# A fused retention and expert kernel: first values by a second queue, the first expert's start moved into the last tiles, rank tables moved later

## The chip, the cores and the metric

One core of one Trainium2 chip. Its engines are named as the profile names them: PE is TensorE (matrix products), PEld its weight loads, DVE is VectorE, ACT is ScalarE, POOL is GpSimd, and SP issues most DMAs. The metric is the device time of one execution in microseconds (us).

## The reference

```python
# attention: 8 batches x 8 heads x 576 positions x 64
scores = (1/sqrt(64)) * q @ k^T
ret    = (scores * gamma[h] ** (i - j) where i >= j, else 0) @ v
x      = ret as [4608 tokens, 512]
# experts: 4 groups of 4, one of 16 for each token
g_idx  = argmax(x @ w_group);          g_w = its softmax weight
e_idx  = argmax(x @ w_expert[g_idx]);  e_w = its softmax weight
out[token] = g_w * e_w * (relu(x[token] @ w1[g, e]) @ w2[g, e])   # 512 -> 1024 -> 512
```

All in float32. Each token goes to exactly one of the 16 experts.

## The kernel before, in words

The work has two phases. In the first, 36 tiles of 128 tokens (`NT`) pass through the attention. For a tile t, `loads` brings `a` (q and k, transposed) and `b` (k and v), 512 KB each, six tiles ahead; `scale` multiplies the values by the decay on ACT (`vs`); `scores` makes `pss`, which DVE masks into `sT`; `av` makes `px` from `sT` and `vs`; `state` adds to the running state `pst`, copied to `st` by ACT; `inter` adds the state's share to `px`; `turned` scales it on DVE into `xT`, the tokens in transposed form. Tiles are routed in groups of three (`RG`): `logits` (`plt`), `gate_pe` (transposed logits, `pl`), `choose` (a chain of small DVE operations from `lg` to `ob`, the chosen expert as a one-hot row), `places_pe` and `places` (the row in the expert's list, `sl`), `weigh` (the gate weight, `wt`). `xnat` then transposes a tile back (`pxt`), scales it (`xt`) and scatters its rows to the expert's list `xs` in DRAM, by an indirect DMA of POOL.

In the second phase the experts follow one another, in order of their token counts. Pass p has eight steps f: `layer1` makes a 128-wide piece `ph` of the hidden layer, ACT makes `hh` of it, and `layer2` of the step before adds to the outputs `py`. Weights come in four pieces for each expert (`load_piece`, two DMAs `r` of 512 KB). They and the tokens are split into a high and a low part (`wh` on ACT, `wl` on DVE) for three products; the first six steps of pass 0 use whole float32 weights instead (`whole`). `xload` reads an expert's tokens from `xs` (`xb`, four DMAs and the ids) and must wait until all scatters so far have landed, that of `xpad` (rows of zeros behind the list) too. `xturn` transposes them on DVE (`xTf`), `xsplit` splits them (`xTh`, `xTl`). The outputs are transposed on DVE (`yturn`) and scattered by POOL (`ystore`, `finish`).

The first expert is chosen before all tiles are counted: `PICK` is tile 26, and with r = t - 26 the loop calls `pick(0)` at r = 5, `taken` and `xload(0)` at r = 6 and the weights' pieces at r = 6 to 9. Its first 256 tokens (`EARLY`) are pass 0; the rest of its tokens are a last pass 16. The remaining routing of the last tiles is mixed into pass 0, and `rank_experts` ranks all experts by count in three parts, taken one at a time by `next(ranks, None)`.

The order of the work on every engine is the order in which the code calls it: `Ordered` pins each instruction behind the one before on its engine. What is written in another order runs in another order. Only the reads of a register (`expert_of`) aren't pinned. Every recorded operation has the line of that helper, L117, so the rows are read by the names of tiles.

```python
        Ordered.on = True
        act.dma_start(cf[:, 0:KC_UP], c_f[:, 0:KC_UP])
        act.activation(warm, warm, AF.Exp)
```

Of the kernel before, what the change touches and what calls it, by code (L numbers as in the profile page):

```python
# [15 lines left out]
P = 128  # L16
# [50 lines left out]
def moe_retention(ctx, tc, qk, kv, wgt, w1, w2, c_f, out):  # L67
# [262 lines left out]
    def xnat(t):  # L330
        xnat_pe(t)
        xnat_out(t)
        xnat_store(t)

    def xnat_pe(t):

        T = tiles[t]
        T["pxt"] = ps_tr.tile([P, NKC, P], F32, name=f"pxt_{t}", tag="tr")
        for i in range(NKC):
            pe.transpose(T["pxt"][:, i, :], T["xT"][:, i, :], ident)  # L340
# [181 lines left out]

    obs = []
# [3 lines left out]
    with ExitStack() as ac:  # L527
# [7 lines left out]
        def loads(t, nms):  # L535
# [52 lines left out]
        for t in range(LOADS - 1):  # L588
# [137 lines left out]
        for t in range(NT + 1):  # L726
# [22 lines left out]
            if t:  # L749
                inter(t - 1)  # L750
                turned(t - 1)
# [6 lines left out]
            if now and 6 <= t:  # L758
# [9 lines left out]
            u = t - 6  # L768
# [3 lines left out]
            for u in range(max(u + 1, 0), t - 5):  # L772
# [74 lines left out]

    def layer1(p, f):
        i = p * NPIECE + f // 2
        C = CS[p]  # L850
        if (p, f) == (0, 0):
            ph = ps_st.tile([P, CMAX], F32, name=f"ph_{p}_{f}", tag="tr")
        elif p == 0:
            ph = psy.tile([P, CMAX], F32, name=f"ph_{p}_{f}", tag=f"py{f % 2}")
        else:
            pool_ = (ps_sm, ps_tr, ps_sm, ps_st)[f % 4]
            ph = pool_.tile([P, CMAX], F32, name=f"ph_{p}_{f}", tag="sm" if f % 2 == 0 else "tr")
        cs = slice((f % 2) * P, (f % 2) * P + P)
        hh = mp.tile([P, CMAX], F32R, name=f"hh_{p}_{f}", tag="hh", bufs=4)
        if whole(p, f):  # L860
            for kc in range(NKC):
                pe.matmul(
                    ph[:, :C], raws[i][0][:, kc, cs], xTf[p][:, kc, :C], start=kc == 0, stop=kc == NKC - 1
                )
            act.activation(hh[:, :C].bitcast(F32), ph[:, :C], AF.Relu)
            hts[p, f] = (hh.bitcast(F32), None)
            return
        wh, wl = wsp[i, 0]
        xh, xl = xTs[p]
        n = 0  # L870
        for kc in range(NKC):
            for a, b in ((wh, xh), (wh, xl), (wl, xh)):
                pe.matmul(
                    ph[:, :C], a[:, kc, cs], b[:, kc, :C], start=n == 0, stop=n == 3 * NKC - 1
                )
                n += 1
        C32 = 32 * nblocks(p)
        if f == 0 and C32 > C and not natural(p):

            dve.memset(hh[:, C:C32].bitcast(F32), 0.0)  # L880
        hl = mp.tile([P, CMAX], F32R, name=f"hl_{p}_{f}", tag="hl", bufs=4)
        act.activation(hh[:, :C], ph[:, :C], AF.Relu)
        dve.scalar_tensor_tensor(
            hl[:, :C], ph[:, :C], 0.0, hh[:, :C].bitcast(F32), ALU.max, ALU.subtract
        )
        hts[p, f] = (hh, hl)
# [98 lines left out]
    for p in range(E):  # L985
        for f in range(NFC):
# [5 lines left out]
            for i in new:  # L992
                if i not in raws and (i >= len(pieces) or pieces[i][0] in ereg):
                    load_piece(i)
            layer1(p, f)
            if (p, f) == (0, 0):
# [370 lines left out]
```

## Time and profile before

| | |
|---|---|
| three runs | 609.99 us median, 607.59 to 610.55 |
| the profiled execution | 606.85 us |
| its span, first to last instruction | 605.1 us |
| PE busy | 584.0 us, 97% of the span |
| DVE, ACT, POOL busy | 430.2, 325.2, 263.3 us |
| mean DMA rate | 237 GB/s |

A share of the span is an average over stages with different limits. Here PE is nearly always busy; where it is not, the wait has to be looked up at its place. Stretches of the timeline are given in us from the start of the span: the tiles take the first 150 us, pass 0 lasts until about 182, the last pass begins at about 584.

### The profile page before, as it was taken

Reading aid. Unit: us, or ns where it says so; the run is one execution under the profiler, and the core shown is the slowest. Engines: PE = TensorE matmul, PEld = TensorE weight load, DVE = VectorE, ACT = ScalarE, POOL = GpSimd, SP = SyncE. Lnnn points to the kernel's source line nnn. Section 1 sums busy time; section 2 is a strip of 40 time slices with the busy share of each in tenths; the row PEclk is TensorE's granted clock in tenths of the full one; section 3 lists DMA queues with packets and bytes.
Section 4 is the critical chain, followed back from the end, with each engine's and each line's share of the span. In section 5 each row is a group of like instructions: output and inputs, shape, how many; then the busy total and the mean of one; then the engine's idle time right before and its main releaser. Section 6 shows DMA issues by size and latency. Waiting matters only on the chain.

```text
span 605.1 us, 16614 instructions
## 1 busy us (share of the span) xinstructions
PE 584.0 (97%) x6191; PEld 549.7 (91%) x6191; DVE 430.2 (71%) x977; ACT 325.2 (54%) x849; POOL 263.3 (44%) x392
## 2 busy tenths in 40 slices
PE   7889999998999999999999999999999999999995
PEld 7778788777668999999999999999999999999994
DVE  3777677677477666997757675867768677686773
ACT  4677877865346434445435454544545455455553
POOL 0022322333313037494645537373563734636554
PEclk8999999999999999999999999999999999999999
DMA  8999999956983942819465563838467394674921
GB/s 332 416 384 341 344 344 337 353 183 194 381 261 97 349 199 77 298 40 340 111 265 146 230 235 145 284 115 311 130 245 249 123 334 118 259 240 153 369 93 35
DMA packets 62546, 143.11 MB, mean 237 GB/s; under 512 B 9313, under 2 KB 30185, under 8 KB 62464
## 3 DMA queue, kind: packets, MB, share of 16 engines
q1 hardware_dynamic: 53072, 121.59, 57.1%
q0 software_dynamic: 9248, 20.35, 9.4%
q8 instruction: 49, 0.80, 0.5%
q14 instruction: 33, 0.27, 0.1%
q10 hardware_dynamic: 144, 0.10, 0.1%
HBM read 121.67 MB, written 24.88 MB: 242 GB/s over the span
## 4 chain that ended last, share of the span: by engine, by line
PE 87%; DMA 5%; DVE 2%; issue 2%; POOL 1%; ACT 1%; SPq 0%; POOLq 0%; ACTq 0%; DVEq 0%
PE py L117 34%; PE ph L117 34%; PE px L117 7%; PE pss L117 4%; PE pxt L117 3%; PE pst L117 2%; DMA b<-in_kv 2%; PE plt L117 2%; POOL out L117 1%; DMA r<-in_w 1%; DMA xb<-xs 1%; DMA a<-in_qk 1%; PE pl L117 1%; DMA xs<-xt,sl 1%; PE phn L117 0%
## 5 line engine op out<-in xcount | busy, mean ns | idle before, releaser
L117 POOL DMA_INDIRECT out<-y,ii x152 | 167.2, 1100 | 51.0 <-issue 33.8
L117 DVE TENSOR_TENSOR wl<-r,wh 128x512 fp32r<-128x512 f32 x260 | 167.8, 687 | 8.3 <-ACT wh L117 4.5
L117 ACT ACTIVATE hh<-ph 128x356 fp32r<-128x356 f32 (+16 forms) x128 | 53.8, 420 | 212.6 <-PE ph L117 143.1
L117 PE MATMUL ph<-xTh_m,wh 128*128 128x356 f32 (+15 forms) x488 | 147.5, 302 | 0.8 <-ACT xTh_m L117 0.8
L117 ACT CAST wh<-r 128x512 fp32r<-128x512 f32 x260 | 146.9, 617 | 0.0
L117 PE MATMUL ph<-xTl_m,wh 128*128 128x356 f32 (+15 forms) x488 | 146.7, 301 | 0.1
L117 PE MATMUL ph<-xTh_m,wl 128*128 128x356 f32 (+15 forms) x488 | 146.6, 300 | 0.0
L117 PE MATMUL py<-hh,wh 128*128 128x288 f32 (+17 forms) x480 | 145.1, 302 | 0.0
L117 PE MATMUL py<-hl,wh 128*128 128x356 f32 (+14 forms) x480 | 144.7, 301 | 0.0
L117 PE MATMUL py<-hh,wl 128*128 128x356 f32 (+14 forms) x480 | 144.6, 301 | 0.0
L117 DVE SCALAR_TENSOR_TENSOR hl<-ph,hh 128x356 fp32r<-128x356 f32 (+15 forms) x122 | 56.7, 465 | 103.0 <-ACT hh L117 69.9
L117 POOL COPY pace<-hh 1x1 f32<-1x1 f32 x140 | 34.6, 247 | 140.4 <-ACT hh L117 138.4
L117 PEld LDWEIGHTS ph<-xTh_m,wh 128*128 128x128 f32 x488 | 92.0, 189 | 1.7 <-ACT xTh_m L117 1.2
L117 PEld LDWEIGHTS ph<-xTl_m,wh 128*128 128x128 f32 x488 | 92.0, 189 | 0.9 <-DVE xTl_m L117 0.4
L117 PEld LDWEIGHTS ph<-xTh_m,wl 128*128 128x128 f32 x488 | 92.2, 189 | 0.0
L117 PEld LDWEIGHTS py<-hh,wh 128*128 128x128 f32 x480 | 90.5, 189 | 0.2
L117 PEld LDWEIGHTS py<-hl,wh 128*128 128x128 f32 x480 | 90.4, 188 | 0.2 <-DVE hl L117 0.2
L117 PEld LDWEIGHTS py<-hh,wl 128*128 128x128 f32 x480 | 90.5, 189 | 0.0
L117 POOL DMA_INDIRECT xs<-xt,sl x36 | 35.9, 998 | 119.5 <-DVE ob L117 47.1
L117 ACT ACTIVATE vs<-b,cf 128x64 f32<-128x64 f32 x288 | 72.4, 335 | 7.9 <-DMA b<-in_kv 7.9
L117 DVE TENSOR_TENSOR sT<-pss,masks 128x512 f32<-128x512 f32 x72 | 46.0, 681 | 15.9 <-PE pss L117 10.7
L117 PE MATMUL px<-sT,vs 128*64 128x128 f32 x576 | 40.1, 280 | 2.2 <-DVE xT L117 1.7
(167 smaller groups left out, 615.8 us busy)
## 6 DMA issues: line engine op xcount, KB each, us to landing
r<-in_w SPq DMA_DIRECT2D x138, 512.0 KB
a<-in_qk SPq DMA_DIRECT2D x35, 512.0 KB
b<-in_kv SPq DMA_DIRECT2D x35, 512.0 KB
xb<-xs SPq DMA_DIRECT2D x24, 148.5 KB
xb<-xs SPq DMA_DIRECT2D x20, 165.0 KB
out<-y,ii POOLq DMA_INDIRECT x152
xb<-xs SPq DMA_DIRECT2D x12, 181.5 KB
xb<-xs SPq DMA_DIRECT2D x4, 198.0 KB
```

The costliest lines, as they stand in the source:

```text
L117: i_ = f(*a, **k)
```

## The change

It moves work; no product is added or removed.

- Start: the first tile's values (`b` of tile 0, two DMAs) are issued by ACT instead of SP, the second half first. The factors `gqs` go behind tile 1's loads, the gate's weights `wgp` and the second part of the constants `cf` behind tile 3's.
- Choice of the first expert: tile 26's `xnat` moves to r = 5, ahead of `pick(0)`'s product, into another PSUM pool. Weight pieces are loaded at r = 5 to 8, the first ahead of the tokens' read; the tokens are transposed at r = 8.
- First product: `layer1(0, 0)` moves into the loop, between tile 34's `inter` and `turned`. Its `hh` lies in a weight buffer. `layer1` itself moves up in the file.
- Pass 0: the routing of the last tiles is distributed otherwise over its steps; `layer2(0, 5)` goes ahead of `layer1(0, 6)`; the padding for the second expert is scattered before the last two tiles.
- Second and third part of the ranking move to the steps (1, 0) and (1, 1), and with them `ids(1)`, `xpad(2)` and `xload(2)`.
- End: one more split of the last pass's weights is called ahead of the last full pass's `layer2`.

```diff
+    def xnat_pe(t, pool_=None):
+        T["pxt"] = (pool_ or ps_tr).tile(
+            [P, NKC, P], F32, name=f"pxt_{t}", tag="sm" if pool_ else "tr"
+        )
...
+        if (p, f) == (0, 0):
+            hh = wp.tile([P, NKC, EARLY], F32, name="hh_0_0", tag="wl0", bufs=3)[:, 0]
...
                     for i in range(2):
-                        sp.dma_start(T[nm][:, i], src[nm][t, :, i])
+                        if nm == "a":
+                            sp.dma_start(T[nm][:, i], src[nm][t, :, i])
+                        else:
+                            act.dma_start(T[nm][:, 1 - i], src[nm][t, :, 1 - i])
...
-            if t == 0:
+            if t == 1:
                 sp.dma_start(gqs[0], c_f[:, KC_GQ:KC_ALL].rearrange("p (x j) -> p x j", x=4))
-            if t == 1:
+            if t == 3:
                 sp.dma_start(wgp, wgt.rearrange("p (c e) -> p c e", c=NKC))
                 sp.dma_start(cf[:, KC_UP:KC], c_f[:, KC_UP:KC])
...
                 inter(t - 1)
+                if r == 9:
+                    layer1(0, 0)
                 turned(t - 1)
...
-            if now and 6 <= t:
+            if now and 6 <= t and r != 6:
                 xnat_pe(t - 6)
                 xnat_out(t - 6)
...
+            if r == 5:
+                xnat_pe(PICK, ps_sm)
+                xnat_out(PICK)
             if now and last_of_group(t - 4):
                 places_pe(t - 4)
...
-            if r in (6, 7, 8, 9):
+            if r in (5, 6, 7, 8):
                 if r == 6:
                     xload(0)
-                load_piece(r - 6)
-            if r == 9:
+                load_piece(r - 5)
+            if r == 8:
                 xturn(0, 0, 2)
                 xturn(0, 1, 2)
...
+            ahead = (p, f) == (0, WHOLE)
+            if ahead:
+                layer2(*prev)
             layer1(p, f)
-            if (p, f) == (0, 0):
+            if (p, f) == (0, 1):
                 places_pe(NT - 4)
                 places(NT - 4)
                 logits(NT - 1)
                 xnat(NT - 6)
-                xnat(NT - 5)
-                gate_pe(NT - 1)
                 pick(1)
-            if (p, f) == (0, 1):
                 expert_of(1)
-                choose(NT - 1)
+            if (p, f) == (0, 2):
                 xnat(NT - 4)
-            if (p, f) == (0, 2):
                 places_pe(NT - 1)
                 places(NT - 1)
                 weigh(NT - 1)
-                xnat(NT - 3)
             if (p, f) == (0, 3):
-                xnat(NT - 1)
+                xnat(NT - 2)
+                count_experts()
+                xnat(NT - 1, ps_sm)
                 xload(1)
...
+            if (p, f) == (0, 1):
+                gate_pe(NT - 1)
+                choose(NT - 1)
+                xnat(NT - 5)
             if (p, f) == (0, 2):
+                xnat(NT - 3)
                 tiles_counted()
-                xnat(NT - 2)
-                count_experts()
-            if (p, f) in ((0, 4), (0, 5)):
+            if (p, f) in ((0, 4), (1, 0), (1, 1)):
                 next(ranks, None)
...
+            if (p, f) == (1, 1):
+                ids(1)
...
+            if (p, f) == (1, 2):
+                xpad(2)
+            if (p, f) == (1, 3):
+                xload(2)
...
         if pc == 0:
 
+            split(2 * E * NPIECE + 3)
             layer2(*prev)
...
-            split(2 * (E * NPIECE + pc) + 3 + k)
+            split(2 * (E * NPIECE + pc) + 4 + k)
```

On SP, at the start of the program, the first loads stand in this order; a and b are a tile's two loads (a_134 and b_136 of before are a_133 and b_135 now, tile 1), gq, wgp and cf the constants.

```order
-L117 DMA b_130<-in_kv 128x512 x2
+L117 DMA a_133<-in_qk 128x1024
+L117 DMA b_135<-in_kv 128x1024
 L117 DMA gq_113<-c_f 128x512
-L117 DMA a_134<-in_qk 128x1024
-L117 DMA b_136<-in_kv 128x1024
+L117 DMA a_138<-in_qk 128x1024
+L117 DMA b_140<-in_kv 128x1024
+L117 DMA a_142<-in_qk 128x1024
+L117 DMA b_144<-in_kv 128x1024
 L117 DMA wgp<-in_wgt 128x128
 L117 DMA cf<-c_f 128x517
```

Tile 0's b is gone from SP, gq stands behind tile 1, and wgp and cf stand behind tiles 2 and 3.

On PE, from tile 34's first product on, before:

```order
L117 MATMUL px_3089<-sT_2979,vs_2917 64x128 x8
L117 MATMUL px_3089<-a_2456,st_2943 64x128 x8
L117 MATMUL pxt_3107<-cf,xT_2494 128x128 x4
L117 MATMUL pl_3114<-cf,lt_3075 128x128 x3
L117 MATMUL px_3145<-sT_3060,vs_3006 64x128 x8
L117 MATMUL px_3145<-a_2537,st_2652 64x64 x8
L117 MATMUL px_3145<-a_2537,st_3032 64x64 x8
L117 MATMUL ph_0_3193<-xTf_3128,r_0_0_2899 128x256 x4
```

and now:

```order
L117 MATMUL px_3098<-sT_2983,vs_2921 64x128 x8
L117 MATMUL px_3098<-a_2456,st_2947 64x128 x8
L117 MATMUL ph_0_3115<-xTf_3095,r_0_0_2824 128x256 x4
L117 MATMUL pxt_3123<-cf,xT_2494 128x128 x4
L117 MATMUL pl_3130<-cf,lt_3079 128x128 x3
L117 MATMUL px_3152<-sT_3064,vs_3010 64x128 x8
L117 MATMUL px_3152<-a_2537,st_2652 64x64 x8
L117 MATMUL px_3152<-a_2537,st_3036 64x64 x8
L117 MATMUL ph_1_3200<-xTf_3095,r_0_0_2824 128x256 x4
```

The product ph_0 stood behind both products of tile 35 and stands ahead of tile 29's transposes now; the second product, ph_1, has taken its old place.

On DVE, at the end of the last full pass (hl_7 is its last hidden piece, wl_16_1 are lower halves of the last pass's weights, y its transposed output):

```order
 L117 SCALAR_TENSOR_TENSOR hl_7_9235<-ph_7_9221,hh_7_9222 128x260
 L117 TENSOR_TENSOR wl_16_1_9239<-r_16_1_8991,wh_16_1_9238 128x512 x2
-L117 STREAM_TRANSPOSE y_9283<-py_0_8967 128x9x32
-L117 STREAM_TRANSPOSE y_9283<-py_1_8968 128x9x32
-L117 STREAM_TRANSPOSE y_9283<-py_2_8969 128x9x32
-L117 STREAM_TRANSPOSE y_9283<-py_3_8970 128x9x32
-L117 TENSOR_TENSOR wl_16_1_9316<-r_16_1_8992,wh_16_1_9315 128x512 x2
+L117 TENSOR_TENSOR wl_16_1_9257<-r_16_1_8992,wh_16_1_9256 128x512 x2
+L117 STREAM_TRANSPOSE y_9289<-py_0_8967 128x9x32
+L117 STREAM_TRANSPOSE y_9289<-py_1_8968 128x9x32
+L117 STREAM_TRANSPOSE y_9289<-py_2_8969 128x9x32
+L117 STREAM_TRANSPOSE y_9289<-py_3_8970 128x9x32
```

A split of two halves, which stood behind the four transposes, stands ahead of them.

## Rows read from the trace of the kernel before

**Rows 1.** Busy time of each engine in five stretches, us from the start of the span.
```profile
7.58:13.00 5.42, 5.31 (x78) 4.69 (x80) 1.70 (x3) 3.90 (x16) 0.00 (x0) 0.69 1.04 411
...
144.50:150.00 5.50, 4.13 (x87) 3.27 (x85) 3.00 (x8) 1.58 (x4) 2.37 (x4) 1.00 1.02 305
...
150.00:155.00 5.00, 4.17 (x31) 2.97 (x32) 2.60 (x14) 1.55 (x3) 0.00 (x0) 1.00 1.03 403
...
180.00:186.00 6.00, 4.91 (x23) 3.39 (x21) 5.45 (x12) 4.77 (x11) 0.00 (x0) 1.00 0.12 49
...
200.00:484.00 284.00, 284.00 (x1984) 283.81 (x1984) 208.38 (x408) 135.31 (x291) 150.82 (x218) 1.00 0.59 203
```

**Rows 2.** Timeline of the first tiles: start, duration, engine, operation, [idle before <- releaser].
```profile
1.66 0.90 SPq L117 DMA_DIRECT2D b<-in_kv  x2
...
13.59 2.02 ACT L117 ACTIVATE vs<-b,cf 128x64 f32<-128x64 f32 x8 [1.05 <-DMA b<-in_kv]
...
15.91 0.69 PE L117 MATMUL pst<-vs,b 128*64 128x64 f32 x16 [0.79 <-ACT st L117]
...
19.16 2.02 ACT L117 ACTIVATE vs<-b,cf 128x64 f32<-128x64 f32 x8 [0.18 <-DMA b<-in_kv]
...
21.09 0.35 ACT L117 COPY st<-pst 128x256 f32<-128x256 f32 x1
...
22.06 0.65 PE L117 MATMUL pst<-vs,b 128*64 128x64 f32 x16
```

**Rows 3.** Timeline from the choice of the first expert to its first product.
```profile
131.58 0.18 PE L117 MATMUL pc<-ob,ones 128*128 128x16 bf16 x1
...
135.39 0.43 PE L117 MATMUL px<-sT,vs 128*64 128x128 f32 x2 [0.39 <-DVE xT L117]
...
137.90 0.99 POOL L117 DMA_INDIRECT xs<-xt,sl  x1 [2.00 <-ACT xt L117]
...
141.39 1.92 SPq L117 DMA_DIRECT2D xb<-xs  x4
...
145.33 0.67 PE L117 MATMUL px<-a,st 64*64 64x128 f32 x16
...
147.47 1.29 DVE L117 STREAM_TRANSPOSE xTf<-xb 128x512 f32<-128x512 f32 x2
...
148.69 0.37 DVE L117 TENSOR_REDUCE lg<-pl 128x60 f32<-128x240 f32 x1
...
150.00 1.97 PE L117 MATMUL ph<-xTf,r 128*128 128x256 f32 x8 [0.67 <-DMA r<-in_w]
...
150.49 0.68 DVE L117 TENSOR_TENSOR xT<-px,gq 128x512 f32<-128x512 f32 x1
```

**Rows 4.** Timeline of the last scatters and of the second expert's tokens.
```profile
161.43 1.88 PE L117 MATMUL py<-r,hh 128*128 128x512 f32 x4
...
164.35 0.99 POOL L117 DMA_INDIRECT xs<-xt,sl  x1 [3.27 <-ACT xt L117]
...
168.89 1.13 POOL L117 DMA_INDIRECT xs<-xt,sl  x1 [0.28 <-issue]
...
172.90 1.89 SPq L117 DMA_DIRECT2D xb<-xs  x4
...
181.77 0.43 PE L117 MATMUL ph<-xTh_m,wh 128*128 128x356 f32 x1 [0.76 <-ACT xTh_m L117]
```

**Rows 5.** The costliest groups of the page: here the lower halves of the weights.
```profile
L117 DVE TENSOR_TENSOR wl<-r,wh 128x512 fp32r<-128x512 f32 x260 | 167.8, 687 | 8.3 <-ACT wh L117 4.5
```

**Rows 6.** Timeline of the end of the program.
```profile
583.91 1.57 DVE L117 STREAM_TRANSPOSE y<-py 128x288 f32<-128x288 f32 x4
...
585.76 0.97 POOL L117 DMA_INDIRECT out<-y,ii  x1 [6.34 <-DVE y L117]
...
597.31 0.97 POOL L117 DMA_INDIRECT out<-y,ii  x1 [0.30 <-issue]
...
599.61 0.97 POOL L117 DMA_INDIRECT out<-y,ii  x1 [1.33 <-ACTq L1182]
```

More of the change, by code (lines that the diff above doesn't have):

```diff
@@ L521, in without, with layer1 @@
         dve.tensor_scalar(mi0, sln, picked["c0"], float(BIG), ALU.is_ge, ALU.mult)
+    def layer1(p, f):
+        i = p * NPIECE + f // 2
+        C = CS[p]
+        if (p, f) == (0, 0):
+            ph = ps_st.tile([P, CMAX], F32, name=f"ph_{p}_{f}", tag="tr")
+        elif p == 0:
+            ph = psy.tile([P, CMAX], F32, name=f"ph_{p}_{f}", tag=f"py{f % 2}")
+        else:
+            pool_ = (ps_sm, ps_tr, ps_sm, ps_st)[f % 4]
+            ph = pool_.tile([P, CMAX], F32, name=f"ph_{p}_{f}", tag="sm" if f % 2 == 0 else "tr")
+        cs = slice((f % 2) * P, (f % 2) * P + P)
+        if (p, f) == (0, 0):
+            hh = wp.tile([P, NKC, EARLY], F32, name="hh_0_0", tag="wl0", bufs=3)[:, 0]
+        else:
+            hh = mp.tile([P, CMAX], F32R, name=f"hh_{p}_{f}", tag="hh", bufs=4)
+        if whole(p, f):
+            for kc in range(NKC):
+                pe.matmul(
+                    ph[:, :C], raws[i][0][:, kc, cs], xTf[p][:, kc, :C], start=kc == 0, stop=kc == NKC - 1
+                )
+            hf = hh if f == 0 else hh.bitcast(F32)
+            act.activation(hf[:, :C], ph[:, :C], AF.Relu)
+            hts[p, f] = (hf, None)
+            return
+        wh, wl = wsp[i, 0]
+        xh, xl = xTs[p]
+        n = 0
+        for kc in range(NKC):
+            for a, b in ((wh, xh), (wh, xl), (wl, xh)):
+                pe.matmul(
+                    ph[:, :C], a[:, kc, cs], b[:, kc, :C], start=n == 0, stop=n == 3 * NKC - 1
+                )
+                n += 1
+        C32 = 32 * nblocks(p)
+        if f == 0 and C32 > C and not natural(p):
+            dve.memset(hh[:, C:C32].bitcast(F32), 0.0)
+        hl = mp.tile([P, CMAX], F32R, name=f"hl_{p}_{f}", tag="hl", bufs=4)
+        act.activation(hh[:, :C], ph[:, :C], AF.Relu)
+        dve.scalar_tensor_tensor(
+            hl[:, :C], ph[:, :C], 0.0, hh[:, :C].bitcast(F32), ALU.max, ALU.subtract
+        )
+        hts[p, f] = (hh, hl)
     obs = []
@@ L771, in moe_retention @@
                 u -= 1
-            for u in range(max(u + 1, 0), t - 5):
+            for u in range(max(u + 1, 0), t - 5 + (r == 5)):
                 if now:
@@ L845, in rank_experts @@
         dve.tensor_scalar(mil, el, cr[:, 0:1], float(BIG), ALU.is_ge, ALU.mult)
-    def layer1(p, f):
-        i = p * NPIECE + f // 2
-        C = CS[p]
-        if (p, f) == (0, 0):
[L852 to L886, printed above, removed]
     def layer2(p, f):
@@ L1025, in moe_retention @@
                 split(2 * pc + f % 2 + 3)
-            if prev is not None:
+            if not ahead:
                 layer2(*prev)
-                if f == 0:
-                    for i in range(NKC if p > 1 else 2):
-                        yturn(p - 1, i) if p > 1 else finish(0, i)
+            if f == 0:
+                for i in range(NKC if p > 1 else 2):
+                    yturn(p - 1, i) if p > 1 else finish(0, i)
+            if (p, f) == (0, 1):
+                gate_pe(NT - 1)
+                choose(NT - 1)
+                xnat(NT - 5)
             if (p, f) == (0, 2):
+                xnat(NT - 3)
                 tiles_counted()
-                xnat(NT - 2)
-                count_experts()
-            if (p, f) in ((0, 4), (0, 5)):
+            if (p, f) in ((0, 4), (1, 0), (1, 1)):
                 next(ranks, None)
@@ L1038, in moe_retention @@
                 expert_of(2)
-            if (p, f) == (0, 7):
-                next(ranks, None)
+            if (p, f) == (1, 1):
+                ids(1)
             if p > 1 and f > 0:
@@ L1046, in moe_retention @@
                     ystore(p - 1, b)
-            if f == (4 if p > 0 else 7) and p + 2 <= E:
+            if (p, f) == (1, 2):
+                xpad(2)
+            if (p, f) == (1, 3):
+                xload(2)
+            if f == 4 and p and p + 2 <= E:
                 xpad(p + 2)
-            if f == (5 if p > 0 else 7):
+            if f == 5 and p:
                 xload(p + 2)
@@ L1061, in moe_retention @@
                     xsplit(p + 1, kc)
-            if f == NFC - 1 and p + 1 < E:
+            if f == NFC - 1 and 0 < p < E - 1:
                 ids(p + 1)
```

13 lines of the change are left out of this document (7 added, 6 removed).

## The prediction

> **What bounds the kernel now.** I read the busy time by stretches first, to find where TensorE is not busy. From 200 to 484 us it is busy for all 284.00 us; the changed code has the same products there, so that part is a constant. Idle time is found at the seams: 5.50 - 4.13 = 1.37 us before 150, 5.00 - 4.17 = 0.83 us up to 155, and 6.00 - 4.91 = 1.09 us between 180 and 186 [rows 1]. Then the timeline of each seam tells what ends last.
>
> Start: at 7.58 to 13 us the DMA engines are full (share 1.04, 411 GB/s) [rows 1]. ScalarE scales a tile's values as soon as they land: those of tile 2 at 13.59, after a wait for the DMA, of tile 4 at 19.16, again after one. The state product at 15.91 waits for a copy on ScalarE that is queued behind this scaling. At 22.06 the same product waits for nothing: its copy ran from 21.09 to 21.44 [rows 2]. So up to tile 3 the landing of the values sets the pace, and from tile 4 on TensorE with VectorE does.
>
> First seam, 131 to 155: the expert is chosen from the counts at 131.58 (pc), VectorE's chain of small operations follows, and TensorE waits at 135.39 for a result behind it. The scatter of tile 26 is issued at 137.90, its landing lets SP read the expert's tokens at 141.39, and SP issues the weights after these; the first product starts at 150.00 after 0.67 us of waiting for weights [rows 3].
>
> Second seam, 164 to 186: the last three tiles are scattered from 164.35 to 168.89, SP reads the second expert's tokens at 172.90, and the second pass's first product waits for them until 181.77 [rows 4]. What TensorE saves earlier in the first pass is worth nothing unless these tokens come earlier too.
>
> End: VectorE transposes the last full expert's output at 583.91, and from 585.76 GpSimd issues nine scatters, the last at 597.31. It is then free at 598.28. The program's final scatter starts at 599.61 after 1.33 us of idle time [rows 6].
>
> **The change part by part.** *Constants later.* The order shows that wgp (128x128) and the rest of cf (128x517) move behind tile 3's loads: (128 + 517) x 128 x 4 bytes = 0.330 MB, at 411 GB/s [rows 1] 0.80 us. Tile 2's and 3's values land 0.80 us earlier, and so do the state products that wait for them. By tile 4 as many bytes stand ahead as before. Its scaling still starts at 19.16, its copy still ends at 21.44, and the product after that now starts at 22.06, so at most 22.06 - 21.5 = 0.56 us can be kept. I take 0.55; the ends are 0 (a late landing at tile 3 or 4) and 0.80. The gate's weights are needed only after tile 2's group, so moving them costs nothing; the products of the first tiles cover them, and without that cover the gate's first product would wait up to the same 0.80 us.
>
> *First values from ScalarE's queue.* This moves two issues of 0.90 us together off SP [rows 2], and SP's next loads are issued that much earlier. But the engines behind the queues are full, and what binds is tile 2 to 4, whose bytes are the same. So I cost it at 0; the cover is the full DMA, and without it the gain could reach the 0.90 us. It can't lose on the path either: if ScalarE issues them late, after its table load, tile 0's products are late, while everything up to tile 2's landing has room. The Trainium skill ("DMA: Bandwidth & Descriptors", section "Issuing engines are not separate DMA queues") says that transfers issued by several engines run on the same DMA engines, and that a second issuer saves only the issue time. By that rule the sum would get 0.90 us here; the row with share 1.04 says that even this buys nothing.
>
> *Tile 26 and the first weights earlier.* Tile 26's four transposes move ahead of pc, by one iteration. The chain behind pc starts later by them: I have no row for exactly these, and bound them by 0 and the 0.67 us of the sixteen small products at 145.33 [rows 3]. Since TensorE has little else there, I take 0.3 us of loss. In return the scatter of tile 26 is issued before the padding's, whose rows come from the chain behind pc: that chain is over before 135.39 + 0.67 = 136.1, and with 141.39 - 137.90 = 3.49 us from scatter to read, SP reads the tokens by 139.6 instead of 141.39. The weights' first piece no longer stands behind that read, so the 0.67 us wait for weights goes.
>
> *First product moved ahead of tile 35's.* TensorE is free for it at 145.33 + 0.67 = 146.00. The tokens' read to the start of their transposes took at most 147.47 - 141.39 = 6.08 us; from 139.6 that is 145.7, plus 1.29 for the transposes 147.0 at the latest. So it starts between 146.0 and 147.0 instead of 150.00. What is late next is the second product: the order puts it right behind tile 35, and its bank (with the counts behind it) waits for VectorE's choice for tile 32 and tile 35's xT. That stretch took from 148.69 to 150.49 + 0.68 = 151.17 [rows 3]. It can begin only after tile 32's logits are transposed, now behind the first product, thus between 146.0 + 1.97 = 148.0 and about 148.7. So the second product starts at 150.5 to 151.2. Before, the first one started at 150.00: one product of 1.97 us is gained and 0.5 to 1.17 us lost, 0.8 to 1.5 us net. I take 1.1, less the 0.3 above: 0.8 us on TensorE.
>
> *Last scatters.* The second seam takes of this only what the tokens of expert 1 take. The transposes of tile 33, the first of the last three scatters, now stand behind one more second product (1.88 us [rows 4]), and the padding's scatter, one more issue on GpSimd, stands before the last two instead of before the last: the number of issues between 164.35 and 168.89 is the same. Ends: nothing, or the whole 0.8 us and a little for a DMA that has fewer weights left to load. I take 0.5 us. SP's loads of the third expert's weights move ahead of its tokens; both are needed some 25 us later.
>
> *Rank tables.* Their two parts run on VectorE between 180 and 188 or earlier now, and move by a few us into the second pass, where TensorE is busy throughout [rows 1] and VectorE is not. Costed at nothing; the third expert's tokens are then read about 4 us later, some 5 us before they are transposed. If that cover were gone, each us late would stall one.
>
> *The last weights' split.* One split of two halves, 2 x 0.687 = 1.37 us [rows 5], now stands on VectorE ahead of the output transposes. The row of these shows no idle time ahead of them, so GpSimd's nine scatters start 1.37 us later. Their room is 1.33 us less the usual gap of 0.30: 1.03 us [rows 6]. What is left over, 1.37 - 1.03 = 0.34, goes to the end; ends 0 and 1.37. I take 0.3. TensorE's own waits in the tail get shorter, but GpSimd ends last.
>
> **Sum.** -0.55 - 0.5 + 0.3 = -0.75 us. The profiled execution took 606.85 us (a span of 605.1 and 1.75 around it), so it becomes 606.1. The runs' median is 609.99, 0.5% above the profiled one; the mean of these four executions is 608.75, and from that I forecast 608.0.
>
> **Rivals.** *The waits at both seams go.* If the second expert's tokens come as early as TensorE is ready, all of 1.37 + 0.83 + 1.09 = 3.29 us goes, with 0.80 at the start and a free end: -4.1, 604.65. For it speaks that DMA has little to do before 144 and SP can load weights then; against it, that the tokens need the last scatter, whose transposes were moved behind another product.
>
> *Slower: the transposes of the first tokens block VectorE.* They now stand in VectorE's queue ahead of tile 34's xT, and tile 35's products wait for that. If the tokens are read no earlier than now, because their read waits for the padding's scatter and shares the DMA with the first weights, the transposes end at 147.47 + 1.29 = 148.76, and TensorE waits from 146.0. First product, tile 35 and VectorE's chain then follow one another: 2.76 late, 1.4 us after today's order, and 0.8 for the chain, +2.2. With -0.55 and +0.3 that is +2.0: 610.7. It decides from about 147.2 on, where the gain of the seam is used up. Against it speaks the 1.8 us by which the read moves forward.
>
> *The change doesn't do what it says.* The early start is given back at the full DMA, and the tokens of expert 1 come when they came: 0 to +0.3, 608.9.
>
> **How the numbers follow.** Forecast 0.58, everything gone 0.22, blocked VectorE 0.10, nothing 0.10. The forecast's own range is -2.0 to +0.5, or 606.7 to 609.3. The range that leaves out 2 in 10 takes in most of the first rival and of the second: 604.4 to 610.3. A change of 0.5% is 3.05 us, about what a measurement of this kernel can tell from none: only the first rival reaches that, and a tail of the forecast: faster 0.25, slower 0.07 (the worse end of the blocked queue), same 0.68.
>
> **What would show it.** Right: the state product of tile 4 about 0.5 us earlier but the scaling at the same 19.16; the tokens' read at about 139.6; the first product at 146 to 147; a wait of about 1 us before the second, ended by VectorE; the last scatter's start only 0.2 to 1 us earlier than 168.89; GpSimd's nine scatters about 1.3 us later relative to the last output's products, and the final scatter directly behind them. Wrong: a last scatter 2 us earlier, or a wait of over 1 us before the first product.

## The result

The changed kernel takes 613.82 us (median of 20 runs, 611.24 to 617.88) against 609.54 us of the kernel before (20 runs, 606.13 to 613.65). The ratio is 1.0076, 95% interval 1.0059 to 1.0093: by the ratio it is 4.6 us slower, where I forecast 608.0 us and gave 0.07 to slower.

The profiled execution took 615.3 us, its span is 613.5 us. The two profiled executions stand farther apart than the medians, and part of that is not the change: the product `plt` of tiles 27 to 29, a little ahead of the choice of the first expert, starts at 130.79 us before and at 132.43 us now. Over the fourteen profiles of this study it starts between 130.69 and 139.01 us, and the latest is that of a kernel whose code up to there is the one of before. So the seams are counted from this row, in the timeline of the kernel before:

```profile
130.79 0.85 PE L117 MATMUL plt<-xT,wgp 128*32 128x384 f32 x8
```

and of the changed kernel:

```profile
132.43 0.85 PE L117 MATMUL plt<-xT,wgp 128*32 128x384 f32 x8
```

Busy time from this product to the first product `py` in the second pass that runs at full pace, for the kernel before (columns as in [rows 1]: stretch, its length, busy time of PE, PEld, DVE, ACT, POOL, granted clock, DMA share, GB/s):

```profile
130.79:188.14 57.35, 52.89 (x528) 39.12 (x528) 40.54 (x138) 29.39 (x76) 16.41 (x28) 1.00 0.68 230
```

and for the changed kernel:

```profile
132.43:196.09 63.66, 55.65 (x528) 41.60 (x528) 40.87 (x130) 29.18 (x76) 17.29 (x28) 0.95 0.70 241
```

The same 528 products: TensorE is idle 57.35 - 52.89 = 4.46 us before and 63.66 - 55.65 = 8.01 us now, and busy for 55.65 - 52.89 = 2.76 us longer, at a mean granted clock of 0.95 instead of 1.00. That is 3.55 + 2.76 = 6.31 us in these two executions. The stretches of the changed kernel that answer to those of [rows 1] show both:

```profile
144.50:150.00 5.50, 4.93 (x109) 3.42 (x104) 4.65 (x11) 3.80 (x12) 2.22 (x4) 1.00 0.94 222
150.00:155.00 5.00, 4.32 (x63) 3.59 (x63) 2.40 (x8) 1.32 (x3) 1.14 (x3) 1.00 1.02 395
155.00:160.00 5.00, 3.80 (x17) 2.87 (x21) 1.70 (x8) 0.08 (x1) 0.19 (x1) 0.66 0.65 267
180.00:186.00 6.00, 5.75 (x34) 4.38 (x32) 3.78 (x9) 0.49 (x2) 0.00 (x0) 1.00 0.95 204
186.00:190.00 4.00, 1.09 (x5) 0.84 (x6) 3.14 (x6) 1.76 (x5) 0.00 (x0) 1.00 1.02 418
190.00:195.00 5.00, 5.00 (x21) 4.47 (x20) 5.00 (x12) 4.71 (x10) 0.60 (x1) 0.66 0.53 215
```

Two stretches run at a mean granted clock of 0.66, 155 to 160 and 190 to 195 us. So part of each runs at the lower of the two levels (1.2 GHz instead of 2.4), the half clock below, and each comes behind a wait. The lower clock is not one of this profiled execution alone: the granted clock of a whole execution is 0.9915 on the mean over the 20 runs of the changed kernel, and 0.9943 to 0.9962 for the kernel before in the three batches of the experiments. It doesn't order all kernels, though: ends, which loses nothing that can be measured, has 0.9932. The waits, of the changed kernel between 129 and 200 us (total, times, longest):

```profile
PE ph L117 <- ACT xTh_m L117: 3.0, 1, 3.0
PE ph L117 <- DVE xT L117: 1.9, 1, 1.9
PE px L117 <- DVE xT L117: 1.1, 2, 0.8
PE pc L117 <- ACT lt L117: 0.7, 1, 0.7
```

**The first seam** (answers to [rows 3]), timeline of the changed kernel; start, duration, engine, and the idle time before in brackets:

```profile
134.02 0.47 ACT L117 COPY lt<-plt 128x384 f32<-128x384 f32 x1
134.54 0.17 PE L117 MATMUL pc<-ob,ones 128*128 128x16 bf16 x1 [0.67 <-ACT lt L117]
136.58 0.99 POOL L117 DMA_INDIRECT xs<-xt,sl  x1 [0.28 <-POOL xt L117]
137.88 0.97 POOL L117 DMA_INDIRECT xs<-zero,pad  x1 [0.30 <-issue]
137.89 0.78 SPq L117 DMA_DIRECT2D r<-in_w  x2
143.60 1.89 SPq L117 DMA_DIRECT2D xb<-xs  x4
148.54 1.31 DVE L117 STREAM_TRANSPOSE xTf<-xb 128x512 f32<-128x512 f32 x2 [0.66 <-DMA xb<-xs]
149.95 1.97 PE L117 MATMUL ph<-xTf,r 128*128 128x256 f32 x8 [0.57 <-issue]
153.63 0.69 PE L117 MATMUL px<-a,st 64*64 64x64 f32 x32
154.42 0.21 DVE L117 TENSOR_TENSOR ob<-oh 128x48 bf16<-128x48 f32 x1
155.45 0.69 DVE L117 TENSOR_TENSOR xT<-px,gq 128x512 f32<-128x512 f32 x1 [0.82 <-PE px L117]
156.20 3.63 PE L117 MATMUL ph<-xTf,r 128*128 128x256 f32 x8 [1.87 <-DVE xT L117]
```

The choice's product `pc` starts 2.11 us behind `plt` (before: 131.58 - 130.79 = 0.79): tile 26's transposes stand ahead of it, and it waits 0.67 us for ScalarE's `lt`. The padding's scatter goes out at 137.88, the first weights (`r`, 1 MB) at 137.89, and the read of the tokens only at 143.60: 5.72 us from the last scatter to the read, where [rows 3] have 3.49. SP itself has issued the weights by 137.89 + 0.78 = 138.67, so the read does not wait for that issue. The first product starts at 149.95, 17.52 us behind `plt` (before 19.21), and tile 35's products still stand behind it. The second product waits 1.87 us for tile 35's `xT` and then takes 3.63 us for the eight matrix products that took 1.97 us just before.

**The second seam** (answers to [rows 4]), the weights of the second expert among the scatters of tiles 30 to 35, their tokens' read and the second pass's start:

```profile
162.89 0.99 POOL L117 DMA_INDIRECT xs<-xt,sl  x1 [7.70 <-DVE e1i L117]
163.69 3.71 SPq L117 DMA_DIRECT2D r<-in_w  x6
166.10 0.99 POOL L117 DMA_INDIRECT xs<-xt,sl  x1 [2.02 <-ACT hh L117]
167.75 0.99 POOL L117 DMA_INDIRECT xs<-xt,sl  x1 [0.45 <-issue]
170.10 0.99 POOL L117 DMA_INDIRECT xs<-xt,sl  x1 [1.16 <-ACT xt L117]
173.18 0.15 POOL L117 IOTA xt<- 128x16 int32 x1 [2.09 <-DMA xs<-xt,sl]
176.84 1.07 POOL L117 DMA_INDIRECT xs<-xt,sl  x1 [0.30 <-issue]
179.78 1.91 SPq L117 DMA_DIRECT2D xb<-xs  x4
188.78 0.43 PE L117 MATMUL ph<-xTh_m,wh 128*128 128x356 f32 x1 [3.04 <-ACT xTh_m L117]
190.60 0.50 PE L117 MATMUL ph<-xTh_m,wl 128*128 128x356 f32 x1
196.09 0.34 PE L117 MATMUL py<-hh,wh 128*128 128x384 f32 x1
```

GpSimd's iota at 173.18 writes the `xt` of tile 34. There are three such buffers, so it waits for the landing of tile 31's scatter, issued at 166.10: 7.08 us, with 3 MB of weights issued from 163.69 on. The last scatter starts 44.41 us behind `plt` (before 168.89 - 130.79 = 38.10), the tokens' read 47.35 us (42.11), the second pass 56.35 us (50.98) after a wait of 3.04 us instead of 0.76. From there to the `py` at 196.09 it takes 7.31 us, before 188.14 - 181.77 = 6.37, with products of 0.50 us among those of 0.33.

Before, two of the last six scatters were out when the weights' issue began, and the third followed 1.24 us later; now one was out, and the next three followed 2.41, 4.06 and 6.41 us later:

```profile
155.01 0.99 POOL L117 DMA_INDIRECT xs<-xt,sl  x1 [5.28 <-ACT xt L117]
156.59 0.99 POOL L117 DMA_INDIRECT xs<-xt,sl  x1 [0.39 <-issue]
158.07 4.25 SPq L117 DMA_DIRECT2D r<-in_w  x6
159.31 0.99 POOL L117 DMA_INDIRECT xs<-xt,sl  x1 [1.53 <-ACT xt L117]
160.94 0.15 POOL L117 IOTA xt<- 128x16 int32 x1 [0.63 <-DMA xs<-xt,sl]
```

The last row shows that a scatter lands slowly before, too: the iota of tile 33 waits for the landing of tile 30's scatter, 160.94 - 155.01 = 5.93 us. There the wait is 0.63 us, and the iota of tile 34 has none.

**Start and end** (answer to [rows 2] and [rows 6]):

```profile
18.87 2.02 ACT L117 ACTIVATE vs<-b,cf 128x64 f32<-128x64 f32 x8 [0.99 <-DMA b<-in_kv]
21.74 0.73 PE L117 MATMUL pst<-vs,b 128*64 128x64 f32 x16
27.79 0.56 PE L117 MATMUL pss<-a 64*64 64x128 f32 x15 [1.20 <-issue]
...
593.28 1.57 DVE L117 STREAM_TRANSPOSE y<-py 128x288 f32<-128x288 f32 x4
595.13 1.48 POOL L117 DMA_INDIRECT out<-y,ii  x1 [7.49 <-DVE y L117]
608.07 0.97 POOL L117 DMA_INDIRECT out<-y,ii  x1 [0.30 <-issue]
```

Tile 4's state product starts at 21.74 instead of 22.06. At 27.79 TensorE goes on after a pause of 1.20 us in the middle of the scores of a tile. Before, the same pause is shorter and ends at the same place, so nothing of the start is left by then:

```profile
27.74 0.56 PE L117 MATMUL pss<-a 64*64 64x128 f32 x15 [0.91 <-issue]
```

The lower halves of the weights take what they took in [rows 5]; it is their place that matters at the end:

```profile
L117 DVE TENSOR_TENSOR wl<-r,wh 128x512 fp32r<-128x512 f32 x260 | 167.8, 687 | 10.6 <-ACT wh L117 6.1
```

VectorE's output transposes start 0.75 us behind the first product `phn` of the last pass (592.53), where they started 0.46 us ahead of it (583.91 and 584.37).

### The profile page after: what moved, and what is told of

It reads as the page before. It is cut to its first block, busy times and chain, and to the rows that moved or that the text cites. A ratio compares the mean times of both kernels' runs of the same rounds, so it can differ in the third digit from the quotient of the medians.

```text
span 613.5 us, 16608 instructions
## 1 busy us (share of the span) xinstructions
PE 587.8 (96%) x6191; PEld 553.0 (90%) x6191; DVE 431.2 (70%) x977; ACT 325.1 (53%) x849; POOL 263.3 (43%) x392
## 4 chain that ended last, share of the span: by engine, by line
PE 89%; DVE 3%; DMA 3%; issue 2%; POOL 1%; ACT 1%; another core or an unknown queue 0%; SPq 0%; ACTq 0%; POOLq 0%; DVEq 0%
PE ph L117 34%; PE py L117 34%; PE px L117 9%; PE pss L117 4%; PE pxt L117 3%; PE pst L117 2%; PE plt L117 2%; DMA xs<-xt,sl 1%; DMA b<-in_kv 1%; POOL out L117 1%; DMA xb<-xs 1%; PE phn L117 1%; DVE xT L117 1%; PE pl L117 1%; DVE sT L117 0%
## 5 line engine op out<-in xcount | busy, mean ns | idle before, releaser
L117 PEld LDWEIGHTS px<-sT,vs 128*64 128x64 f32 x576 | 31.6, 139 | 13.1 <-issue 8.6
```

Of the source, the lines that this page charges most:

```text
L117: i_ = f(*a, **k)
```

## The experiments

All were timed beside the kernel before on the same chip. Places are starts of rows behind that of `plt` in each kernel's profile, in us, one profile for each kernel. "pc" is the product for the choice of the first expert; "pace" is the first `py` on full pace in the second pass.

| kernel | ratio to before, 95% interval | pc | first tokens' read | last scatter | second tokens' read | wait at the second pass | pace |
|---|---|---|---|---|---|---|---|
| before | 1 | 0.79 | 10.60 | 38.10 | 42.11 | 0.76 | 57.35 |
| changed | 1.0076 (1.0059 to 1.0093) | 2.11 | 11.17 | 44.41 | 47.35 | 3.04 | 63.66 |
| ends | 1.0013 (0.9991 to 1.0035) | 0.79 | 10.95 | 38.69 | 42.53 | 1.32 | 58.54 |
| ranks | 1.0006 (0.9984 to 1.0028) | 0.79 | 10.77 | 37.50 | 42.28 | 1.91 | 58.87 |
| pass0 | 1.0058 (1.0037 to 1.0079) | 0.79 | 10.81 | 40.75 | 43.62 | 2.11 | 59.81 |
| first | 1.0040 (1.0022 to 1.0058) | 2.11 | 11.07 | 40.58 | 44.28 | 0.59 | 59.68 |
| weights_behind | 1.0055 (1.0038 to 1.0072) | 2.11 | 7.90 | 43.33 | 46.19 | 3.61 | 62.67 |
| tile26_late | 1.0068 (1.0044 to 1.0093) | 0.78 | 12.13 | 48.69 | 51.60 | 3.01 | 68.70 |
| first_late | 1.0049 (1.0033 to 1.0066) | 2.09 | 10.89 | 41.51 | 44.44 | 3.51 | 60.62 |
| r1_late | 1.0007 (0.9991 to 1.0024) | 2.10 | 11.20 | 42.20 | 45.07 | 1.49 | 61.25 |
| both_behind | 0.9991 (0.9972 to 1.0010) | 2.08 | 7.86 | 39.73 | 42.92 | 1.37 | 58.65 |
| both_behind_late | 0.9974 (0.9954 to 0.9994) | 2.05 | 7.83 | 38.51 | 41.70 | 0.95 | 57.03 |
| pass0_r1 | 0.9965 (0.9943 to 0.9988) | 0.79 | 11.12 | 38.37 | 41.32 | 0.54 | 56.48 |
| before_r1 | 0.9985 (0.9964 to 1.0007) | 0.78 | 10.97 | 38.34 | 41.44 | 0.55 | 57.40 |

### The change in four parts, each alone on the kernel before

**ends**: the start's hunks and the end's one.

```diff
+                            act.dma_start(T[nm][:, 1 - i], src[nm][t, :, 1 - i])
...
-            if t == 1:
+            if t == 3:
                 sp.dma_start(wgp, wgt.rearrange("p (c e) -> p c e", c=NKC))
...
+            split(2 * E * NPIECE + 3)
             layer2(*prev)
```

> The kernel before with two parts of the change alone: the start (tile 0's values issued by ACT, gq, wgp and cf behind later tiles) and the end (one split ahead of the last full output). Theory A, the loss lies at the two seams around pass 0: no measurable change here, 0 to +0.5 us; the state product of tile 4 may come early, but by tile 5 (about 30 us) nothing is left of it, and the end is some 0.3 us longer. Theory C, the loss begins in the tiles, since the profile of the changed kernel already runs 1.64 us late at tile 30: +1.6 us or more here, with TensorE behind at 118 us.

No measurable difference. Tile 4's state product starts at 21.98, tile 6's, at 29.59, within 0.05 us of before. At the end, the last scatter starts 15.53 us behind the first product `phn` of the last pass (601.17 - 585.64), before 15.24 (599.61 - 584.37): 0.3 us. Theory C has no support in the profile: `plt` starts at 130.69 us, 0.10 us earlier than before. The interval by itself reaches to +2.1 us.

**ranks**: the later ranking with `ids(1)`, `xpad(2)` and `xload(2)`.

```diff
-            if (p, f) in ((0, 4), (0, 5)):
+            if (p, f) in ((0, 4), (1, 0), (1, 1)):
                 next(ranks, None)
...
+            if (p, f) == (1, 3):
+                xload(2)
```

> The kernel before with only the second and third part of the ranking, ids(1), xpad(2) and xload(2) moved to the second pass. Theory A (loss at the seams, by other parts): within 0.5 us of before, no new wait of TensorE after 190 us. Rival: the later read of the third expert's tokens or the small operations among the splits stall the second pass, +1 us or more.

No measurable difference over the runs. Its one profile has 1.91 us of wait at the second pass: VectorE, free of the ranking now, waits 2.74 us for the tokens' DMA ahead of their transposes. Behind this wait the clock falls as well: from the pass's first product to the `py` on full pace it takes 7.34 us, before 6.37.

**pass0**: the routing's new distribution over pass 0, without the early first product.

```diff
-            if (p, f) == (0, 0):
+            if (p, f) == (0, 1):
                 places_pe(NT - 4)
...
+                gate_pe(NT - 1)
+                choose(NT - 1)
+                xnat(NT - 5)
...
+                count_experts()
+                xnat(NT - 1, ps_sm)
                 xload(1)
```

> The kernel before with only the new distribution of the last tiles' routing over pass 0 and layer2(0,5) ahead of layer1(0,6); the first product stays behind tile 35 and the first expert's choice as before. Theory A, the second seam is late because the first one is: at most +1 us, the second expert's tokens read within 1 us of 172.9. Theory B, the new order makes them late by itself (padding ahead of the last two scatters, the scatters waiting for buffers of earlier ones): read at 175 or later and +2 to +4 us.

0.58% or 3.5 us slower; the last scatter 2.65 us later, the second expert's tokens read 1.51 us later (43.62 and 42.11). The time is theory B's size, the read lies between the two theories; this part loses by itself. GpSimd's wait for a buffer is there too, 2.54 us.

**first**: tile 26, the first weights, the transposes and the first product earlier, pass 0's routing as before.

```diff
-            if r in (6, 7, 8, 9):
+            if r in (5, 6, 7, 8):
                 if r == 6:
                     xload(0)
-                load_piece(r - 6)
+                load_piece(r - 5)
...
+                if r == 9:
+                    layer1(0, 0)
```

> The kernel before with only the first seam's part: tile 26 ahead of the choice's product, the first weights ahead of the tokens' read, the first tokens transposed one iteration earlier, the first product between tile 34 and 35; pass 0's routing as before. Theory A: +2 to +5 us: the choice's product about 1.3 us late, over 5 us from the padding's scatter to the tokens' read, the second product waiting for tile 35's xT, and the clock falling behind that wait. Theory B: within 1 us of before.

0.40% or 2.4 us slower, at the low end of theory A. One of its signs is missing: the granted clock stays at 1.00 from 150 to 165 us. So the loss has two sources, and neither theory had it all. Alone, the four parts give 1.17% together, the whole change 0.76%; with intervals of about 0.2% either way for each part, that doesn't show that their losses overlap.

### What in the first seam costs

**weights_behind**: the changed kernel, weights behind the tokens' read.

```diff
-            if r in (5, 6, 7, 8):
+            if r in (6, 7, 8, 9):
                 if r == 6:
                     xload(0)
-                load_piece(r - 5)
+                load_piece(r - 6)
```

> The changed kernel with the first expert's weight pieces issued as before: the first one behind the tokens' read. Theory D (the 1 MB of the first piece shares the DMA engines with the padding's scatter, whose landing the read waits for; 5.7 us in the changed kernel, 3.5 before from the last scatter to the read): the read some 2 us earlier, counted from the products plt before it (9.0 to 9.6 us instead of 11.2), the second product about 2 us earlier, the time 1.5 to 2.5 us below the changed kernel. Rival: the read is late because the choice's product is, and stays at 10.5 to 11.2 us; then the weights come later and the time is the same or up to 1 us longer.

The read moves from 11.17 to 7.90 us, more than theory D asked, with `pc` as late as in the changed kernel:

```profile
137.28 0.98 POOL L117 DMA_INDIRECT xs<-zero,pad  x1 [0.30 <-issue]
139.73 1.93 SPq L117 DMA_DIRECT2D xb<-xs  x4
```

2.45 us from the padding's scatter to the read. So the weights held up the scatter's landing. The second product comes only 0.66 us earlier, since it waits 1.86 us for `xT` much as in the changed kernel, but it runs at full clock:

```profile
154.94 1.99 PE L117 MATMUL ph<-xTf,r 128*128 128x256 f32 x8 [1.86 <-DVE xT L117]
```

That is another 3.63 - 1.99 = 1.64 us. Then the second pass waits 3.61 us: the ratio falls by 0.21%, 1.3 us, and its interval overlaps that of the changed kernel. The tokens' delay was real; of the 0.66 + 1.64 = 2.30 us gained by the end of the second product, 0.99 us are left at the pace, behind the second seam.

**tile26_late**: tile 26 put back behind the choice.

```diff
-            if r == 5:
-                xnat_pe(PICK, ps_sm)
-                xnat_out(PICK)
...
-            u = t - 6 + (r == 5)
+            u = t - 6
```

> The changed kernel with tile 26's transposes and scatter put back behind the choice. Theory E (its transposes take the small PSUM buffer that the choice's product needs, so that this waits for ScalarE's lt): the choice's product 0.8 us behind plt again instead of 2.1 us, padding 1.3 us earlier; the read still waits for tile 26's scatter and for the weights, so 10.5 to 12 us behind plt, and the time changes by -1.3 to +0.5 us. Rival: tile 26's scatter sets the read, which then comes at 12 us or later, +1 us or more.

`pc` is 0.78 us behind `plt` again, so it was the transposes and their buffer that delayed it; the read comes at 12.13 us, as the rival had it, 5.0 us behind tile 26's own scatter, the last one ahead of it. The ratio, 1.0068, can't be told from the changed kernel's. Its profile has a pause of 5.6 us ahead of the first product, in which VectorE waits 5.71 us for the tokens' DMA ahead of their transposes; this execution (618.84 us) is the slowest of six, and the ratio over the runs bears out no such loss.

**first_late**: the first product behind tile 35's again.

```diff
-                if r == 9:
-                    layer1(0, 0)
...
             if (p, f) == (0, 0):
+                layer1(p, f)
                 prev = (p, f)
```

> The changed kernel with the first product put behind tile 35's products again, and all else as changed. Theory F (ahead of tile 35 it pushes xT of tile 35, and with it the second product, behind itself; the 1.9 us of waiting there also bring the half clock in the second product, 1.7 us): no wait over 1 us between the first and the second product, the second no slower than 2 us, and the time 1.5 to 3.5 us below the changed kernel. Rival: the late tokens bind both, and the time stays within 1 us.

No wait between the two products and no half clock there (10.00 us busy from 150 to 160, granted clock 1.00). The ratio falls by 0.27%, about 1.6 us, at the low end of theory F, the intervals overlapping; the second pass now waits 3.51 us and loses part of it again.

### What in the second seam costs

**r1_late**: the changed kernel, two of the second expert's weight pieces behind the read of its tokens. It is one line:

```diff
-                new = {2: (4, 5), 3: (6,), 5: (7,)}.get(f, ())
+                new = {2: (4,), 4: (5, 6), 5: (7,)}.get(f, ())
```

> The changed kernel with two of the second expert's weight pieces (2 MB) issued behind the read of its tokens instead of ahead of it. Theory G (the last scatters land late, up to 7 us after their issue, because those weights fill the DMA engines, and a buffer of xt comes free that late): GpSimd's wait of 2.1 us ahead of tile 34's scatter mostly goes, the second expert's tokens are read 2 to 3 us earlier counted from the second product, and the wait at the second pass's start falls from 3.0 to below 1.5 us: -1 to -3 us, unless the weights are then late. Rival: the scatters are late because their transposes are; the read moves by less than 0.7 us and the time by less than 1 us.

1.0007: of the 0.76% only 0.07% is left. Tile 34's iota waits for no landing any more, the tokens' read comes 21.20 us behind the second product instead of 23.58, and the second pass starts after 1.49 us and then runs on at full clock (6.40 us to its `py`):

```profile
166.39 0.99 POOL L117 DMA_INDIRECT xs<-xt,sl  x1 [2.02 <-ACT hh L117]
170.39 0.99 POOL L117 DMA_INDIRECT xs<-xt,sl  x1 [1.16 <-ACT xt L117]
171.40 0.19 POOL L117 IOTA xt<- 128x16 int32 x1
174.88 0.97 POOL L117 DMA_INDIRECT xs<-xt,sl  x1 [0.30 <-issue]
177.75 2.25 SPq L117 DMA_DIRECT2D xb<-xs  x4
187.53 0.43 PE L117 MATMUL ph<-xTh_m,wh 128*128 128x356 f32 x1 [1.49 <-ACT xTh_m L117]
```

In the 7.08 us behind the start of tile 31's scatter the DMA share is 1.00 in the changed kernel (166.10 to 173.18) and 0.62 here (166.39 to 173.47), while VectorE runs the same small operations in both up to 170 us. This is theory G, at somewhat more than its size in the time and at its size in the profile. The profile shows 63.66 - 61.25 = 2.41 us of it up to the pace; it is of the slowest of the twelve runs (613.13 us, their median 609.82), and what the others gain beyond that no profile shows.

**pass0_r1**, **before_r1**: the same line in the run pass0 and in the kernel before.

> The kernel before with only the new distribution of pass 0 (the run pass0, +3.5 us), and two of the second expert's pieces behind the read of its tokens. Theory G: the loss of pass0 was the scatters landing behind those weights; it goes, and the time is within 1 us of before. Theory B (the padding ahead of the last two scatters, later transposes): at least 2 us of the 3.5 stay.

0.9965: the 3.5 us of loss become 2.1 us of gain. Theory B falls: the order of pass 0 costs nothing once the weights don't stand among its scatters, and the kernel is faster than before.

> The kernel before with only two of the second expert's pieces behind the read of its tokens. Theory G: before, the last scatters already share the DMA engines with those weights (share 0.89 from 160 to 180 us), so the read moves forward by up to 1 us, the wait of 0.76 us at the second pass's start goes, unless the moved weights are late: -1 to 0 us. Rival: the weights land too late for the splits, +1 us or more.

0.9985, the interval holds 1: where two of the six scatters are out ahead of the weights and the third soon follows, the line is worth at most 2.2 us. Its interval and that of pass0_r1 overlap, so whether pass 0's new order gains anything over the old one stays open.

**both_behind**, **both_behind_late**: r1_late with weights_behind, and with first_late too.

> The changed kernel with both orders of SP's queue: the first expert's weights behind the read of its tokens, and two of the second expert's pieces behind that of its tokens. Theory G+D (both seams lose to weights that stand ahead of tokens on the DMA engines): the gains add up, r1_late's 4.2 us and 1 to 1.5 us from the first seam, so 608 to 609 us beside 609.3 of before: same or just faster. Rival (the first seam is bound by xT of tile 35, whatever the tokens do): no better than r1_late, 609.8.

> As both_behind, and with the first product behind tile 35's products again. Theory F: what the early first product costs, 1.5 us or so, comes back too: 606.5 to 608 us, faster than before by 1.5 to 3 us. Rival: with tokens early, the early product pays as intended, and moving it back costs up to 1.5 us against both_behind.

0.9991 and 0.9974. With both orders mended the change loses nothing, though the step from r1_late's 1.0007 is too small to tell the first expectation from its rival; with the first product back behind tile 35 there is a small gain. Taken in a square, the weights' order gives 0.85% with the first product early (1.0076 to 0.9991) and 0.75% with it late (1.0049 to 0.9974); the late product gives 0.27% and 0.17%. The first pair is clear; in the second each step's intervals overlap, and only the sign agrees twice. both_behind_late and pass0_r1 are both faster than before, pass0_r1 by 2.1 us; their own order is open.

Two comparisons put the seams side by side. The profiles take the change's losses back one edit at a time: the last scatter starts 44.41 us behind `plt`, then 42.20 (r1_late), 39.73 (both_behind) and 38.51 (both_behind_late), beside 38.10 before. And r1_late differs from pass0_r1 only by the parts first, ranks and ends: 1.0007 to 0.9965, intervals that do not meet. So with the second expert's weights moved these parts still cost 0.42%, 2.6 us, about what first costs alone; r1_late is about as fast as before because pass 0's new order and the moved weights, 0.35% faster in pass0_r1, make up for most of it.

## Why the prediction was wrong

The forecast was -0.75 us and the result is +4.6 us: I expected 0.55 us of gain at the start and 0.5 us at the two seams, and both seams lose. Neither of the two signs of being wrong that I named came (a last scatter 2 us earlier, a wait of over 1 us before the first product): I looked for a bigger gain and for late tokens, not for late scatters.

- **Last scatters** ("Ends: nothing, or the whole 0.8 us ... I take 0.5 us"): this step failed, and cost most. I counted GpSimd's issues, found the same number, and bounded the term by nothing and a gain. The last scatter starts 6.31 us later behind `plt`. r1_late takes 2.21 us of that back, and 0.69% in the time; of the other 4.10 all but 0.41 are gone in both_behind_late, where the first seam is mended too. What costs is shown by r1_late, and by pass0 against pass0_r1: these scatters land slowly while 3 MB of weights are under way, and the new order has tiles 31 and 32 scattered 2.4 and 4.1 us behind the weights' first issue, where they were 1.5 us ahead of it and 1.2 us behind. Nothing in the sum spoke of how long a scatter takes to land, or of the three buffers of `xt` that make a slow landing the next scatter's wait, though the trace of before shows both in a small way, at 160.94 us.
- **Tile 26 and the first weights earlier** ("SP reads the tokens by 139.6"): I took 3.49 us from scatter to read from [rows 3], where no weights stood ahead of it, and used it where I had just moved 1 MB there. It took 5.72 us, and 2.45 us in weights_behind. The choice was 1.32 us late, not 0.3: I bounded it by the transposes alone and missed that their PSUM buffer makes `pc` wait for `lt`. The rival on a blocked VectorE named this sharing as its condition, and its point of decision, a first product later than 147.2, was passed (130.79 + 17.52 = 148.31 in the timeline of before); but its price, 2 us, was added up from late first products and VectorE's chain, and has neither the clock nor the second seam in it.
- **First product ahead of tile 35's** ("0.5 to 1.17 us lost"): right in what ends the wait, wrong in the chain. I put VectorE's small operations ahead of `xT`. They were over at 154.63; what counted was TensorE's own queue behind the first product, to 153.63 + 0.69 = 154.32, then 1.13 us until VectorE starts (the profile puts it down to waiting for this product) and 0.69 us of `xT`: 156.14. And the sum had no term for the clock: the wait of 1.87 us was followed by 3.63 - 1.97 = 1.66 us, the one of 3.04 us by 7.31 - 6.37 = 0.94 us more. These two are 2.60 of the 2.76 us of longer busy time. Instead of the 0.8 us of gain that I took for the first seam, its parts cost 2.4 us by themselves (first), and 0.42% with ranks and ends behind a mended second seam (r1_late against pass0_r1).
- **Constants and first values**: the state product of tile 4 gained 0.32 us, not 0.55 (and 0.08 us in ends, with the same edit), and nothing was left of it by 27.79 us. Its scaling started 0.29 us earlier, at 18.87, where I had it stay at 19.16. The cap that I worked out stopped at tile 4; a cause for the pause that ends at 27.74 and 27.79 us is not in the profile. That the start is worth nothing in the time is within what ends can tell; the second queue by itself was not timed.
- **Rank tables** at nothing: within what ranks can tell (0.9984 to 1.0028), right.
- **The last weights' split** at +0.3: right, with its mechanism. The scatters start 2.60 us behind `phn` (595.13 - 592.53) instead of 1.39, 1.21 us later, and the final scatter follows after 0.30 us instead of 1.33.

The rule of the Trainium skill that I weighed for the start ("DMA: Bandwidth & Descriptors", section "Issuing engines are not separate DMA queues"), that transfers run on the same DMA engines and interleave whoever issues them, is the one that the second seam obeys: GpSimd's scatter needs 7.08 us to land among weights that SP issued. I used it to price an issue at nothing and not to price a landing.

What stays open: whether the early first product still costs some 1 us with early tokens (both_behind against both_behind_late, 0.17%), since the intervals overlap, and why it would. Open, too, is what decides between the two levels of the clock behind a wait of 1.9 us (see the last section).

## What to carry to other kernels

When a bulk load and a small scatter that something waits for meet in time, their order of issue is a term of the sum, even on different queues: price the landing of the scatter with the load ahead of it, and put the load behind the read that waits. A duration taken from the trace holds only with the neighbours that it had there. And where a moved product leaves TensorE idle for a microsecond or two, look at the granted clock behind the gap: the time lost there was almost as long as the gap in one kernel (1.66 us behind 1.87) and nothing in another (weights_behind, behind 1.86).

## What the runs showed of the hardware

A wait of 1.87 us was followed by eight products at about half their pace, 3.63 us for 1.97 (the clock 0.66 on the mean from 155 to 160 us), and one of 3.04 us by 0.50 us products for 0.33. At the second pass the fourteen profiles fall into two groups: in the eight that waited 0.54 to 1.49 us, it took 6.37 to 6.40 us from the pass's first product to the `py` on full pace, all at a granted clock of 1.00; in the six that waited 1.91 to 3.61 us, it took 7.09 to 8.43 us, with 2 us or more of it at a granted clock of 0.50. At the first seam the length of the wait doesn't tell them apart: the second product took 3.63 us behind 1.87 us (changed) and 3.02 us behind 1.86 us (r1_late), but 1.99 us behind 1.86 and 1.85 us (weights_behind, both_behind). In the two slow ones TensorE had also been idle for 0.57 and 0.71 us ahead of the first product, in the two others not; whether that decides is not shown.

The tiles' stretch, 40 to 118 us, where the code is the same, differs between profiles by about as much as the change costs: TensorE was busy there for 75.47 us before and for 70.98 us in pass0, at a DMA share of 0.95 and 0.90; the other twelve lie between 73.71 and 75.63 us. The pauses stand in the middle of runs of equal products and are put down to "issue"; their cause is not in the trace.
